# Six places of a hand-written order moved in a two-problem linear attention kernel

## The chip, the cores and the metric

The kernel runs on one core of one Trainium2 chip. Its time is the device time of one execution in microseconds (us). Engines are named as in the profile: PE multiplies matrices, PEld loads its weights, DVE works on vectors, ACT applies functions element by element and copies, POOL does some element-wise work and issues DMAs, SP issues DMAs. Each engine runs its own instructions in the order in which the program gives them to it, and waits on semaphores for the others.

## The reference, cut to what matters

Two independent problems, A and B, of 2048 tokens with 640 features each; 32 heads of 20 features. The results stand side by side in one output of 2048 x 1280.

```python
qkv = (x @ wqkv).reshape(B, S, 3, H, Dh)...          # q, k, v
phi = lambda t: jnp.where(t > 0, t + 1, jnp.exp(t)) + 1e-6
pq, pk = phi(q), phi(k)
kv  = jnp.einsum("bhsd,bhse->bhde", pk, v)
z   = jnp.einsum("bhsd->bhd", pk)
num = jnp.einsum("bhqd,bhde->bhqe", pq, kv)
den = jnp.einsum("bhqd,bhd->bhq", pq, z)[..., None] + 1e-6
out = concat_heads(num / den) @ wo
```

## The kernel before

**Numbers.** Every large product is made from float32 operands split into a rounded high part and a low part, which is the rest: ACT writes the high part, DVE subtracts it from the source for the low part (`split`, L1024; the subtraction waits in a list and is given to DVE by `flush`, L1019, at the next place of the order). A product is then three matrix products: high x high, high x low, low x high.

**Stages.** In the first half, up to about 283 us, the kernel makes phi(k) of both problems, the sums z, and per problem a 640 x 640 matrix M which holds kv and wo together. This half is ordered by a planner (`Plan`, L78) and is not touched by the change. M is turned into ten "forms" (forms 0 to 9: sums and differences of its blocks, each split high and low), with which an output product takes seven block products instead of eight.

The second half works on quarters of 512 tokens, numbered u = 0 to 7 (0 to 3 are A, 4 to 7 are B; NG = 4, NU = 8). For each quarter: q^T = wq^T x^T (`quarter`, `qmm`; for two quarters of each problem together `pair`, which uses sums of blocks of wq and x^T), phi of it (`qphi`: Exp and Relu on ACT out of a PSUM bank, then DVE; `qacc` adds up the denominators), a division (`divide`), sums of blocks and their splits (`d_sums`, `d_split`, `a_split`), and at last the output product with M (`outmm`). Sums over heads for the denominators go either through PE (`denmm`, quarter 0 alone) or through cross-partition copies, the foldings: `fold1`, `fold3`, `fold5` are copies on ACT, `fold2`, `fold4` additions and reciprocals on DVE.

PE's order in this half, with the start of each part in the profile of before: quarter 0; quarter 1; first part of pair 0, called p0 (326.5); output product 0 (337.0); second part of pair 0, called r0 (352.6); output product 1 (374.2); output product 2 (390.0); quarter 4 (406.9); output product 3 (423.9); quarter 5 (440.8); p1 (457.8); output product 4 (468.1); r1 (485.0); output products 5 (506.5), 6 (522.7) and 7 (538.5).

**The order by hand.** PE's work calls `run(slot)` after each small step, and `at(slot, f, ...)` hangs other work on a slot: `("q", u, c, k)` is after the three products k of column block c of quarter u; `("o", u, s)` is after step s (0 to 13) of output product u; `("p0", i, k)` and the like are steps of a pair. `run` first calls `flush`, then the functions hung there, in the order in which they were hung. A slot sets only the position in each engine's own list: an engine reaches the work when it has done what stands before it, and it may be ahead of PE or behind it.

**An output product** (`outmm`, L1357) has steps n = 0 to 6 for each half q of its 512 tokens. Step n = 0, 2, 4, 5 end with a copy of a PSUM bank into an output tile on ACT (L1396), n = 3, 4, 6 with an addition on DVE (L1397). PE goes on adding to the same bank after the copy, so step 2 waits for the copy of step 0, step 5 for that of step 4, and step 6 for the addition of step 4. The four output tiles `o` have four buffers (bufs=4); POOL (for the last product SP) stores them.

**What the change touches.**
- `chain` (L1662 on): a list per quarter of (slot, function). `chain[0]` is quarter 0 with its `denmm`; `early(b)` (L1667) is the quarter before the last of a problem; `chain[v]` (L1713) is the last quarter of all, v = 7, where `o` is output product 5 and `w` output product 6.
- `round_xq` (L1086): ACT rounds the high part of a piece of x^T for the next quarter from a staging tile; five pieces c = 0 to 4 per quarter. The low parts were made in the first half and are loaded (`load_xq`).
- `z_end` (L712, `finish`): four short DVE operations that finish z of problem B.
- `form_split`, `form_store` (L1145, L1151): six forms of B's M are split into tiles `fs` during quarter 4, stored to memory by POOL (L1156), and later loaded to where A's forms were (`form_load`). The tiles carry the tags `wo0` to `wo3` in turn: two per form, so every second form uses the same pair, and must wait until the store of the form before it in that pair has landed. Their order is 0, 2, 4, 6, 9, 8.
- `steps` (L1721): what a pair needs of wq and x^T. `tw_sums` (POOL) makes block sums of wq, `tw_split` (ACT, then DVE) splits them: `tw_split(b, 1, 1)` and `tw_split(b, 2, 0)` are the entries t[7] and t[9].

```python
parts = [base.tile([P, w], F32R, name=f"fs{t}", tag=turned("wo", 4), bufs=1) for t in "hl"]
o = [[q2[0].tile([P, 2, HF], F32, name="o", tag="o", bufs=4) for _ in range(2)] for _ in range(2)]
```

Of the kernel before, what the change touches and what calls it, by code (L numbers as in the profile page):

```python
# [9 lines left out]
F32R = mybir.dt.float32r  # L10
# [208 lines left out]
def tile_linear_attn_pair(ctx: ExitStack, tc: tile.TileContext, ins, out: bass.AP):  # L219
    nc = tc.nc  # L220
    P = 128
    S, D = ins[0]["x"].shape
    NC = D // P
    NT = S // P
    NG = NT // 4
# [9 lines left out]
    base = ctx.enter_context(tc.tile_pool(name="base", bufs=1))  # L235
# [5 lines left out]
    kx, kg, q1a, q1b, q2, q3 = [], [], [], [], [], []  # L241
# [450 lines left out]
    def zsums(b):  # L692

        z, zt32 = Space("zsum", D, ANY), Space("zturn", D, ANY)
        note("DVE", D, lambda: tt(z.all.f, zac[b][0].all.f, zac[b][1].all.f, op=OP.add), [z.all],
             [x.all for x in zac[b]] + ([G[1, NC - 1].all] if b else []), safe=6.0)
        part, four = Space("zpart", 20), Space("zfour", 20)
        pt, ft4 = zp[b]
        add = dict(axis=mybir.AxisListType.X, op=OP.add)
        note("DVE", D, lambda: nc.vector.transpose(zt32.all.f, z.all.f), [zt32.all], [z.all])  # L700
        note("DVE", D, lambda: nc.vector.tensor_reduce(
            pt.rearrange("p (g c) -> p c g", g=4), zt32.all.f.rearrange("p (c g t) -> p c g t", g=4, t=32), **add),
            [part.all], [zt32.all])
        zdv = Space("zd", 1)
        note("POOL", 1.0, lambda: nc.gpsimd.dma_start(zd[b], pt), [zdv.all], [part.all], dma=0.1, lat=2.0)
        for g in range(4):
            note("POOL", 1.0, lambda g=g: nc.gpsimd.dma_start(
                ft4[g * 32:g * 32 + 32].rearrange("p (q c) -> p q c", q=4),
                zd[b].rearrange("(q i) (g c) -> g i q c", q=4, g=4)[g]), [four[g:g + 1]], [zdv.all], dma=0.1, safe=6.0)
        zt, s = zz[b]  # L710

        def finish():  # L712
            nc.vector.tensor_reduce(zt, ft4.rearrange("p (q c) -> p c q", q=4), **add)
            nc.vector.tensor_scalar(zt, zt, S * EPS, None, op0=OP.add)
            nc.vector.tensor_reduce(s, zt, **add)
            nc.vector.tensor_scalar(s, s, EPS, EPS / 4, op0=OP.mult, op1=OP.add)

        if b == 0:
            note("DVE", 300, finish, [KZ[b].all], [four.all], safe=6.0)
        return finish  # L720
# [181 lines left out]
    for p in range(4, NPB):  # L902
        i, h = divmod(p - 2, 2)
# [9 lines left out]
    for p in range(NPB + 1, NP):  # L913
        if p == NPB + 1:
            fl = kvs
        else:
            i, h = divmod(p - NPB - 2, 2)
# [25 lines left out]
    z_end = zsums(1)  # L943
# [43 lines left out]
    for g, (h0, nh) in enumerate(GROUPS):  # L987
        cols = NC * DH * nh
        w = Space("wv", cols, (BD,))
# [23 lines left out]
    def turned(tag, n):  # L1013
        turn[tag] = (turn.get(tag, -1) + 1) % n
        return f"{tag}{places[turn[tag]] if tag == 'wst' else turn[tag]}"
# [8 lines left out]
    def split(hi, lo, src, now=False):  # L1024
        nc.scalar.activation(hi, src, AF.Copy)
        lows.append((lo, src, hi))
        if now:
            flush()
# [8 lines left out]
    def at(slot, f, *a):  # L1037
        todo.setdefault(slot, []).append((f, a))
# [103 lines left out]
    def width(i):  # L1142
        return D if i < 6 or i == 8 else HF

    def form_split(b, i):  # L1145
        w = width(i)
        parts = [base.tile([P, w], F32R, name=f"fs{t}", tag=turned("wo", 4), bufs=1) for t in "hl"]
        split(*parts, raw.pop((b, i))[:, :w])
        fd[b, i] = parts

# [453 lines left out]
    def forms2(b, places):  # L1604

        for i, a, s in places:
            at(a, form_split, b, i)
            at(s, form_store, b, i)
# [16 lines left out]
    h = NG - 1  # L1625
# [19 lines left out]
    for c in range(NC):  # L1645
        at(("q", 0, 4, c - 1) if c else ("q", 0, 3, 2), split_xq, 1, c, c == NC - 1)
        at(("o", 1, 8 + c // 2) if c < 2 else ("o", 2, c + 2), load_xraw, NG, c)
        at(("o", 1, 4 + c), load_xq, NG, c)
        at(("o", 2, 7 + c), round_xq, NG, c)
        u = NG  # L1650
        if c == 3:
            for k in (1, 3):
                at(("q", u, 3, 2), load_w, "m", 1, k)
        at(("q", u, *((3, 0), (3, 1), (3, 1), (4, 2), (4, 3))[c]), load_xraw, u + 1, c)
        at(("q", u, 4, c), load_xq, u + 1, c)
        at(("o", u - 1, (1, 2, 3, 11, 12)[c]), round_xq, u + 1, c)

    at(("o", 2, 8), z_end)

    den[0] = bank("psd", "small", 1)  # L1660

    chain = {  # L1662
        0: [(("q", 1, 0, 0), split_acc, 0), (("q", 1, 1, 1), denmm, 0), (("q", 1, 1, 1), recip, 0, 0),
            (("q", 1, 1, 1), recip, 0, 1), (("q", 1, 1, 2), divide, 0, 0), (("q", 1, 1, 4), divide, 0, 1),
            (("q", 1, 2, 0), d_sums, 0, 0), (("q", 1, 2, 2), a_split, 0, 0), (("q", 1, 2, 4), d_sums, 0, 1),
            (("q", 1, 3, 1), d_split, 0, 0), (("q", 1, 3, 4), a_split, 0, 1), (("q", 1, 4, 1), d_split, 0, 1)]}
    def early(b):  # L1667
        v = b * NG + NG - 1
        u = v - 1
        o, w, r = ("o", u - 1), ("o", u), (f"r{b}", 5)  # L1670
        y = (f"r{b}", 4)
        return [((*y, 4), phi7, v, 2), ((*y, 3), phi7, v, 3), ((*y, 1), fold1, u), ((*y, 2), fold2, u),
                ((*y, 2), qacc, v, 2), ((*r, 0), fold3, u, 0), ((*r, 0), fold3, u, 1), ((*r, 0), qacc, v, 3),
                ((*r, 1), fold4, u), ((*r, 1), phi7, v, 4), ((*r, 3) if b else (*o, 0), phi7, v, 0), ((*r, 3), qacc, v, 4),
                ((*o, 0) if b else (*o, 1), phi7, v, 1), ((*r, 5) if b else (*o, 1), qacc, v, 0), ((*o, 1) if b else (*o, 2), qacc, v, 1),
                ((*o, 2 - b), fold5, u, 0), ((*o, 2 - b), fold5, u, 1), ((*o, 3 - b), divide, u, 0), ((*o, 4 - b), divide, u, 1),
                *[((*w, n - 14) if n > 13 else (*o, n), f, u, i, q) for n, f, i, q in (
                    (9, d_sums, 0, 0), (10, a_split, 0, 0), (11, d_split, 0, 0), (11, d_sums, 1, 0), (12, a_split, 1, 0),
                    (13, d_split, 1, 0), (14, d_sums, 0, 1), (15, a_split, 0, 1), (16, d_split, 0, 1), (16, d_sums, 1, 1),
                    (17, a_split, 1, 1), (19, d_split, 1, 1))]]  # L1680

    for v in range(1, NU - 2):
# [3 lines left out]
        w, u = v - 1, v + 1  # L1686
# [6 lines left out]
        if v == NU - 3:  # L1693
            p = "p1"
# [14 lines left out]
    u, v = NU - 2, NU - 1  # L1709
    o, w = ("o", u - 1), ("o", u)  # L1710
    chain[u] = early(1)
    e = ("o", v)
    chain[v] = [((*o, 4), fold1, v), ((*o, 5), fold2, v), ((*o, 8), fold3, v, 0), ((*o, 8), fold3, v, 1),  # L1713
                ((*o, 10), fold4, v, 0), ((*w, 4), fold4, v, 1), ((*w, 6), fold5, v, 0), ((*w, 7), fold5, v, 1),
                ((*w, 6), divide, v, 0), ((*w, 7), divide, v, 1),
                *[((*e, n - 14) if n > 13 else (*w, n), f, v, i, q) for n, f, i, q in (
                    (8, d_sums, 0, 0), (9, a_split, 0, 0), (10, d_split, 0, 0), (10, d_sums, 1, 0), (11, a_split, 1, 0),
# [3 lines left out]
    def steps(b, t, x, n0):  # L1721
        p, r, o = f"p{b}", f"r{b}", ("o", b * NG + NG - 4)
        X = [(n0 + i) % 6 for i in range(6)]
        for a, f, *y in ((t[0], tw_load, b, 0), (t[1], tw_sums, b, 0), (t[2], tw_split, b, 0, 0), (t[3], tw_split, b, 0, 1),
                         (t[4], tw_load, b, 1), (t[5], tw_sums, b, 1), (t[6], tw_split, b, 1, 0), (t[7], tw_split, b, 1, 1),
                         ((p, 0, 0), tw_load, b, 2, X[5]), (t[8], tw_sums, b, 2), (t[9], tw_split, b, 2, 0)):
            at(a, f, *y)
        for a, f, *y in ((x[0], xload, 0, 0, X[0]), (x[1], xload, 0, 1, "o"), (x[2], xload, 0, 2, "o"), (x[3], xload, 0, 3, X[1]),
                         (x[4], xload, 0, 4, X[2]), ((p, 0, 0), xsum, 1, 0, X[3]), ((p, 0, 1), xsum, 1, 1, X[4]),
                         ((*o, 0), xsum, 0, 0, X[5]), ((p, 1, 0), xsum, 0, 1, X[0]), ((p, 1, 1), xsum, 2, 0, X[1]),  # L1730
                         ((p, 1, 2), xsum, 2, 1, "w"), ((p, 1, 2), xload, 1, 4, X[2]),
                         ((r, 0, 0), xsum, 3, 0, "o"), ((r, 0, 0), xsum, 3, 1, X[3]), ((r, 0, 1), xload, 0, 4, X[4]),
                         ((r, 1, 0), xload, 1, 3, X[5]), ((r, 1, 1), xload, 1, 0, X[0]), ((r, 1, 1), xload, 1, 1, "o"),
                         ((r, 2, 3), xload, 1, 2, X[1])):
            at(a, f, b, *y)

    p, h = "p1", NU - 3
    X0, X1 = [(turn["xqh"] + 1 + NC * i) % 6 for i in (1, 3)]
    steps(1, (("q", h, 0, 4), ("q", h, 2, 0), ("q", h, 3, 0), ("q", h, 3, 2), ("q", h, 4, 2), (p, 0, 0), (p, 1, 1), (p, 1, 2),
              (p, 1, 0), (p, 1, 2)),  # L1740
          (("q", h, 0, 3), ("q", h, 1, 1), ("q", h, 1, 2), ("q", h, 4, 0), ("q", h, 4, 1)), X1)
    p = "p0"
    steps(0, (("q", 0, 4, 4), ("q", 1, 0, 3), ("q", 1, 1, 2), ("q", 1, 2, 1), ("q", 1, 3, 0), (p, 0, 1), (p, 1, 0), (p, 1, 2),
# [83 lines left out]
```

## Time and profile before

| | before |
|---|---|
| runs (us) | 558.67, 559.19, 560.62 |
| median (us) | 559.19 |
| profiled execution, its own time (us) | 559.77 |
| its span, first to last instruction (us) | 558.0 |
| busy in the span (us): PE, PEld, DVE, ACT, POOL | 550.9, 495.3, 435.7, 355.4, 94.9 |
| granted TensorE clock | 1.00 throughout |

A row of the timeline gives start and duration in us, engine, line of the kernel, operation, out<-in by tile names, sizes, count, and in brackets the idle time of the engine before it with what ended it. Names: `psq`, `psd`, `pa`, `pe`, `psb` are PSUM banks; `xqh` high parts of x^T; `fsh`, `fsl` the split forms and `fdh`, `fdl` their place in memory; `twh`, `twl` split parts of wq; `ac`, `rd` denominators; `o` output tiles. Matrix products overlap in PE, so their pace is read from their starts, not from their durations.

### The profile page before, as it was taken

The numbers are of one execution on the slowest core, as the hardware profiler recorded it, in microseconds if no ns is written. First come the engines' busy times: TensorE is split into PE (matmuls) and PEld (weight loads), VectorE is DVE, ScalarE is ACT, GpSimd is POOL, SyncE is SP. The second block draws the span as 40 slices with busy tenths as digits, with TensorE's granted clock in tenths as the row PEclk, the third lists the DMA queues.
The fourth block names the chain that finished last, engine by engine and source line by source line (L and its number), as shares of the span: only waits on it lengthen the run. The fifth ranks groups of instructions, "written<-read, shape, count | busy, mean of one in ns | idle before, by whom it ended". The sixth has DMA issues, their size and how long they took to land.

```text
span 558.0 us, 9441 instructions
## 1 busy us (share of the span) xinstructions
PE 550.9 (99%) x3342; PEld 495.3 (89%) x3342; DVE 435.7 (78%) x708; ACT 355.4 (64%) x671; POOL 94.9 (17%) x145
## 2 busy tenths in 40 slices
PE   9999999999999999999999999999999999999997
PEld 7999999998998889998887789889988988989997
DVE  7788777579887576978774799779797878959992
ACT  6777476574667656657345557487866856558661
POOL 1210111101211111101214530101333323100110
PEclk9999999999999999999999999999999999999999
DMA  8785998979859989999999979748467986670222
GB/s 317 268 217 168 233 297 228 291 214 280 251 158 258 298 221 314 310 355 286 309 312 272 365 248 323 266 145 288 155 227 241 314 317 208 211 260 1 95 96 94
DMA packets 96359, 135.48 MB, mean 243 GB/s; under 512 B 8248, under 2 KB 54232, under 8 KB 96312
## 3 DMA queue, kind: packets, MB, share of 16 engines
q1 hardware_dynamic: 87000, 108.55, 59.9%
q0 software_dynamic: 9024, 25.94, 17.2%
q8 instruction: 26, 0.43, 0.3%
q10 hardware_dynamic: 288, 0.39, 0.2%
q14 instruction: 21, 0.17, 0.1%
HBM read 79.58 MB, written 44.78 MB: 223 GB/s over the span
## 4 chain that ended last, share of the span: by engine, by line
PE 85%; issue 4%; DMA 3%; ACT 2%; DVE 2%; POOL 2%; SPq 0%; POOLq 0%; ACTq 0%
PE psg L565 20%; PE ka L315 10%; PE pa L1381 10%; PE psq L1526 10%; PE ke L315 5%; PE psr L565 5%; PE pe L1381 5%; PE psk L831 4%; PE psb L1381 3%; PE kb L315 3%; PE psq L1031 2%; PE psq L1032 2%; PE psq L1033 2%; PE pskv L620 1%; PE psm L633 1%
## 5 line engine op out<-in xcount | busy, mean ns | idle before, releaser
L565 PE MATMUL psg<-pkh,xnl 128*128 128x512 f32 x160 | 63.0, 394 | 0.0
L565 PE MATMUL psg<-pkl,xnh 128*128 128x512 f32 x160 | 63.0, 394 | 0.0
L565 PE MATMUL psg<-pkh,xnh 128*128 128x512 f32 x160 | 62.5, 391 | 0.0
L417 POOL DMA_DIRECT2D zacc<-ek x32 | 26.2, 818 | 199.7 <-DVE ek L521 168.9
L511 ACT ACTIVATE kt<-ka 128x320 f32<-128x320 f32 x52 | 22.5, 433 | 55.3 <-PE ka L315 55.1
L1396 ACT ACTIVATE o<-pa 128x320 f32<-128x320 f32 x64 | 27.7, 439 | 30.4 <-PE pa L1381 27.4
L1218 DVE SCALAR_TENSOR_TENSOR pq<-eq,rq 128x512 f32<-128x512 f32 x40 | 28.1, 711 | 11.2 <-ACT rq L1217 11.1
L565 PEld LDWEIGHTS psg<-pkh,xnl 128*128 128x128 f32 x160 | 30.1, 188 | 6.5
L1031 PE MATMUL psq<-xqh,wh 128*128 128x512 f32 x90 | 35.5, 394 | 0.0
L1032 PE MATMUL psq<-xql,wh 128*128 128x512 f32 x90 | 35.2, 391 | 0.0
L1033 PE MATMUL psq<-xqh,wl 128*128 128x512 f32 x90 | 35.1, 390 | 0.0
L565 PEld LDWEIGHTS psg<-pkh,xnh 128*128 128x128 f32 x160 | 30.1, 188 | 4.8
L565 PEld LDWEIGHTS psg<-pkl,xnh 128*128 128x128 f32 x160 | 30.1, 188 | 4.8
L521 DVE SCALAR_TENSOR_TENSOR ek<-ek,kt 128x640 f32<-128x640 f32 x26 | 21.4, 822 | 15.8 <-ACT kt L520 15.8
L412 ACT ACTIVATE pkh<-ek,epst 128x640 fp32r<-128x640 f32 x32 | 26.5, 828 | 6.8 <-DVE ek L521 6.6
L578 DVE TENSOR_TENSOR gacc<-psg,gacc 128x512 f32<-128x512 f32 x30 | 20.6, 688 | 11.0 <-PE psg L565 10.9
L413 DVE SCALAR_TENSOR_TENSOR pkl<-ek,pkh 128x640 fp32r<-128x640 f32 x32 | 26.2, 821 | 3.6 <-ACT pkh L412 3.5
L1229 DVE SCALAR_TENSOR_TENSOR acc<-pq,z,acc 128x512 f32<-128x512 f32 x32 | 26.0, 813 | 1.5 <-ACT acc L1227 0.5
L1434 POOL DMA_DIRECT2D out<-o x14 | 7.7, 549 | 113.7 <-ACT o L1396 81.2
L1381 PE MATMUL pa<-fm,dah 128*128 128x320 f32 x112 | 26.5, 311 | 0.3 <-ACT o L1396 0.3
L309 DVE TENSOR_TENSOR xnl<-xns,xnh 128x640 fp32r<-128x640 f32 x32 | 25.7, 819 | 0.9 <-ACT xnh L306 0.8
L309 DVE TENSOR_TENSOR xl<-xts,xh 128x640 fp32r<-128x640 f32 x29 | 23.8, 821 | 2.7 <-ACT xh L306 2.5
(270 smaller groups left out, 1834.5 us busy)
## 6 DMA issues: line engine op xcount, KB each, us to landing
zacc<-ek POOLq DMA_DIRECT2D x32, 320.0 KB, 5.5
out<-o POOLq DMA_DIRECT2D x28, 320.0 KB, 3.3
xd<-xl SPq DMA_DIRECT2D x24, 320.0 KB, 3.7
xql<-xd SPq DMA_DIRECT2D x26, 256.0 KB, 6.0
xns<-in_A_x SPq DMA_DIRECT2D x16, 320.0 KB, 6.3
xh<-xh SPq DMA_DIRECT2D x16, 320.0 KB, 4.0
xts<-in_B_xt_tiles SPq DMA_DIRECT2D x16, 320.0 KB, 4.4
xns<-in_B_x SPq DMA_DIRECT2D x16, 320.0 KB, 6.8
```

The lines of the kernel that those rows point to most:

```text
L309: note("DVE", n, lambda: tt(lo.r, src.f, hi.f, op=OP.subtract), [lo], [src, hi], ahead=10.0)
L315: nc.tensor.matmul(o, a.r, w.r, start=start and k == i == 0, stop=k == n - 1 and i == 2, skip_group_check=True)
L412: note("ACT", n + 110, lambda: act(hi.r, p.f, AF.Identity, bias=epst), [hi], [p, K0.all], by=8.0)
L413: note("DVE", n, lambda: stt(lo.r, p.f, EPS, hi.f, op0=OP.add, op1=OP.subtract), [lo], [p, hi], by=9.0)
L565: nc.tensor.matmul(o[:, :n], a.r, w.r, start=j == 0 and q == 0, stop=j == 2 and q == 2, skip_group_check=True)
L1031: nc.tensor.matmul(o, whi, xhi, start=first, stop=False)
L1032: nc.tensor.matmul(o, whi, xlo, start=False, stop=False)
L1033: nc.tensor.matmul(o, wlo, xhi, start=False, stop=last)
L1218: nc.vector.scalar_tensor_tensor(pq[u][:, c, :], e, 1.0, r, op0=OP.min, op1=OP.add)
L1381: nc.tensor.matmul(ps, x, y, start=start and n == i == 0, stop=n == len(terms) - 1 and i == 2, skip_group_check=True)
L1396: copy = lambda x, y: nc.scalar.activation(x, y, AF.Copy)
L1526: nc.tensor.matmul(ps, a, z, start=first and i == 0, stop=last and i == 2, skip_group_check=True)
```

## The change

Six places of the order move. Nothing is computed that was not computed before, and no instruction is added or removed.

1. Quarter 0's `denmm` and its two reciprocals go from slot ("q", 1, 1, 1) to ("q", 1, 1, 2), and its first `divide` from there to ("q", 1, 1, 3).
2. The five roundings of quarter 4's x^T go from steps 7, 8, 9, 10, 11 of output product 2 to steps 2, 4, 9, 11, 13; `z_end` goes from step 8 of that product to the second part of p0.
3. Forms 4 and 6 of B are split into two tiles each of the output ring `o` instead of the `wo` tiles; forms 9 and 8 thereby take the `wo` tiles that forms 0 and 2 had.
4. In the last-but-one quarter of B, the second `divide` goes from step 3 to step 7 of output product 5.
5. For the last quarter, in output product 5: `fold1` from step 4 to 3, `fold2` from 5 to 4, the halves of `fold3` from 8 and 8 to 5 and 7, the first half of `fold4` from 10 to 8.
6. `tw_split(1, 1, 1)` and `tw_split(1, 2, 0)` go from the end of p1 to steps 3 and 2 of output product 4.

```diff
     def form_split(b, i):
         w = width(i)
-        parts = [base.tile([P, w], F32R, name=f"fs{t}", tag=turned("wo", 4), bufs=1) for t in "hl"]
+        if b and i in (4, 6):
+            parts = [q2[0].tile([P, D], F32R, name=f"fs{t}", tag="o", bufs=4)[:, :w] for t in "hl"]
+        else:
+            parts = [base.tile([P, w], F32R, name=f"fs{t}", tag=turned("wo", 4), bufs=1) for t in "hl"]
...
-        at(("o", 2, 7 + c), round_xq, NG, c)
+        at(("o", 2, (2, 4, 9, 11, 13)[c]), round_xq, NG, c)
...
-    at(("o", 2, 8), z_end)
+    at(("p0", 1, 0), z_end)
...
-        0: [(("q", 1, 0, 0), split_acc, 0), (("q", 1, 1, 1), denmm, 0), (("q", 1, 1, 1), recip, 0, 0),
-            (("q", 1, 1, 1), recip, 0, 1), (("q", 1, 1, 2), divide, 0, 0), (("q", 1, 1, 4), divide, 0, 1),
+        0: [(("q", 1, 0, 0), split_acc, 0), (("q", 1, 1, 2), denmm, 0), (("q", 1, 1, 2), recip, 0, 0),
+            (("q", 1, 1, 2), recip, 0, 1), (("q", 1, 1, 3), divide, 0, 0), (("q", 1, 1, 4), divide, 0, 1),
...
-... ((*o, 3 - b), divide, u, 0), ((*o, 4 - b), divide, u, 1),
+... ((*o, 3 - b), divide, u, 0), ((*o, 4 + 3 * b), divide, u, 1),
...
-    chain[v] = [((*o, 4), fold1, v), ((*o, 5), fold2, v), ((*o, 8), fold3, v, 0), ((*o, 8), fold3, v, 1),
-                ((*o, 10), fold4, v, 0), ((*w, 4), fold4, v, 1), ...
+    chain[v] = [((*o, 3), fold1, v), ((*o, 4), fold2, v), ((*o, 5), fold3, v, 0), ((*o, 7), fold3, v, 1),
+                ((*o, 8), fold4, v, 0), ((*w, 4), fold4, v, 1), ...
...
-    steps(1, (..., (p, 0, 0), (p, 1, 1), (p, 1, 2),
-              (p, 1, 0), (p, 1, 2)),
+    steps(1, (..., (p, 0, 0), (p, 1, 1), ("o", h - 1, 3),
+              (p, 1, 0), ("o", h - 1, 2)),
```

More of the change, by code (lines that the diff above doesn't have):

```diff
@@ L1675, in early @@
                 ((*o, 0) if b else (*o, 1), phi7, v, 1), ((*r, 5) if b else (*o, 1), qacc, v, 0), ((*o, 1) if b else (*o, 2), qacc, v, 1),
-                ((*o, 2 - b), fold5, u, 0), ((*o, 2 - b), fold5, u, 1), ((*o, 3 - b), divide, u, 0), ((*o, 4 - b), divide, u, 1),
+                ((*o, 2 - b), fold5, u, 0), ((*o, 2 - b), fold5, u, 1), ((*o, 3 - b), divide, u, 0), ((*o, 4 + 3 * b), divide, u, 1),
                 *[((*w, n - 14) if n > 13 else (*o, n), f, u, i, q) for n, f, i, q in (
@@ L1712, in tile_linear_attn_pair @@
     e = ("o", v)
-    chain[v] = [((*o, 4), fold1, v), ((*o, 5), fold2, v), ((*o, 8), fold3, v, 0), ((*o, 8), fold3, v, 1),
-                ((*o, 10), fold4, v, 0), ((*w, 4), fold4, v, 1), ((*w, 6), fold5, v, 0), ((*w, 7), fold5, v, 1),
+    chain[v] = [((*o, 3), fold1, v), ((*o, 4), fold2, v), ((*o, 5), fold3, v, 0), ((*o, 7), fold3, v, 1),
+                ((*o, 8), fold4, v, 0), ((*w, 4), fold4, v, 1), ((*w, 6), fold5, v, 0), ((*w, 7), fold5, v, 1),
                 ((*w, 6), divide, v, 0), ((*w, 7), divide, v, 1),
@@ L1738, in tile_linear_attn_pair @@
     X0, X1 = [(turn["xqh"] + 1 + NC * i) % 6 for i in (1, 3)]
-    steps(1, (("q", h, 0, 4), ("q", h, 2, 0), ("q", h, 3, 0), ("q", h, 3, 2), ("q", h, 4, 2), (p, 0, 0), (p, 1, 1), (p, 1, 2),
-              (p, 1, 0), (p, 1, 2)),
+    steps(1, (("q", h, 0, 4), ("q", h, 2, 0), ("q", h, 3, 0), ("q", h, 3, 2), ("q", h, 4, 2), (p, 0, 0), (p, 1, 1), ("o", h - 1, 3),
+              (p, 1, 0), ("o", h - 1, 2)),
           (("q", h, 0, 3), ("q", h, 1, 1), ("q", h, 1, 2), ("q", h, 4, 0), ("q", h, 4, 1)), X1)
```

## The prediction

> **What bounds the kernel now.** I read the page's busy times first, then the chain of waits in order of time, then the list of who waited for whom on PE, and last the timeline around each of those waits.
>
> ```profile
> PE 550.9 (99%) x3342; PEld 495.3 (89%) x3342; DVE 435.7 (78%) x708; ACT 355.4 (64%) x671; POOL 94.9 (17%) x145
> ```
> ```profile
> 337.00 1.76 PE pa L1381 x12
> ...
> 485.15 21.54 PE psq L1526 x93
> ```
> ```profile
> PE pa L1381 <- ACT o L1396: 0.8, 2, 0.6
> PE pe L1381 <- ACT rq L1217: 0.8, 1, 0.8
> PE psd L1240 <- DVE ac L1022: 0.6, 1, 0.6
> PE pe L1381 <- DVE o L1397: 0.3, 1, 0.3
> ```
>
> The first row says that PE is the bound: 550.9 of 558.0 us. The chain gives its pace: 1.76/12 = 0.147 us from one 320-column product to the next, 21.54/93 = 0.23 us for 512 columns. A product's own row shows 0.31 or 0.39 us, so successive products overlap, and an idle time in brackets is less than what PE loses: I add 0.31 - 0.147 = 0.16 us to it. The last four rows are every wait of PE over 0.15 us behind the start-up. No product is added or removed by the change, so it can gain only what these waits cost, and lose only by new ones.
>
> **The change part by part.**
>
> *First denominators (denmm, recip, divide of quarter 0).*
>
> ```profile
> 312.91 0.39 PE L1239 MATMUL psd<-ac,same 128*128 128x512 f32 x1
> 313.90 0.50 PE L1240 MATMUL psd<-ac,same 128*128 128x512 f32 x1 [0.61 <-DVE ac L1022]
> 314.24 0.39 PE L1031 MATMUL psq<-xqh,wh 128*128 128x512 f32 x1
> ```
>
> The second product comes 0.99 us after the first instead of 0.23: a loss of 0.76. The next comes after 0.34, so refilling PE costs another 0.11; I use that for every wait. The low half of the sums is ready at 313.9 whatever PE does. With denmm one step later, three products (3 x 0.23 = 0.69) stand ahead of it, and 0.07 us of wait stays. The gain is between 0.69 and 0.87, and I take 0.75. The reciprocals start when both sums are in, which is at the same time as now; DVE and ACT therefore do not come earlier here, only PE does. The tw_split's low half now goes ahead of the first divide on DVE, a swap of two operations inside one backlog.
>
> *z_end, out of output product 2 and into the pair's first part (p0).* Four short DVE operations, the first the longest:
>
> ```profile
> 399.62 0.19 DVE L713 TENSOR_REDUCE z<-zq 128x5 f32<-128x20 f32 x1
> ```
> ```profile
> 338.22 0.69 DVE L1218 SCALAR_TENSOR_TENSOR pq<-eq,rq 128x512 f32<-128x512 f32 x1 [0.68 <-ACT rq L1217]
> ```
>
> Four times 0.19 is 0.76 at most. In their new place they run just ahead of the second row, where DVE idles 0.68 us for an ACT result that is paced by PE; that idle time covers them but for 0.1, and it is also where the backlog that the denominators left is worked off. Without this cover the pair's additions would be 0.76 later; I cost it at nothing.
>
> *Roundings of x^T in output product 2.*
>
> ```profile
> 402.99 0.31 PE L1381 MATMUL pe<-fm,dal 128*128 128x320 f32 x1
> 403.57 0.56 PE L1381 MATMUL pa<-fm,dah 128*128 128x320 f32 x2 [0.27 <-ACT o L1396]
> ```
> ```profile
> 400.69 0.84 ACT L1265 ACTIVATE ac<-ac 32x256 f32<-32x256 f32 x2
> 401.56 0.63 ACT L1088 ACTIVATE xqh<-xqs 128x512 fp32r<-128x512 f32 x1
> 402.21 0.84 ACT L1265 ACTIVATE ac<-ac 32x256 f32<-32x256 f32 x2
> 403.08 0.44 ACT L1396 ACTIVATE o<-pa 128x320 f32<-128x320 f32 x1
> ```
> ```profile
> 403.08 0.98 DVE L1270 TENSOR_TENSOR ac<-ac 128x256 f32<-128x256 f32 x1 [1.88 <-ACT ac L1265]
> 404.10 0.95 DVE L1272 RECIPROCAL ac<-ac 128x128 f32<-128x128 f32 x1
> ```
>
> PE loses 0.58 - 0.147 = 0.43 at 403.57, and 0.30 + 0.16 = 0.46 at the next wait, the one on DVE; with two refills that is 1.1 us. ACT runs in order: the copy PE needs stands at 403.08 behind roundings and foldings. The change puts two of the five roundings into steps 2 and 4, so about 2 x 0.63 goes from ahead of these foldings, less a wait for PE in between; the foldings end near 402.05 and the copy near 402.5, before PE's own 402.99 + 0.147 = 403.14. DVE follows: sum and reciprocal (0.98 + 0.95) end near 404.0, the addition behind them near 404.45, and PE wants it after nine products at 404.47. So the first wait goes whole and the second but for 0 to 0.15. The last rounding is now behind the foldings at the product's end; the next quarter uses it only in its fifth part, 12 x 0.23 = 2.8 us later, and it and the half folding ahead of it take 1.5. Gain 0.95 to 1.1; I take 1.0.
>
> *Two M forms in output tiles.*
>
> ```profile
> 422.70 0.61 ACT L1217 ACTIVATE rq<-psq 128x512 f32<-128x512 f32 x1
> 426.05 0.74 ACT L1025 ACTIVATE fsh<-wst 128x640 fp32r<-128x640 f32 x1 [2.75 <-DVE fsl L1022]
> ```
> ```profile
> 428.14 0.42 PE L1381 MATMUL pa<-fh,dsh 128*128 128x320 f32 x1 [0.55 <-ACT o L1396]
> ```
> ```profile
> 419.45 0.54 POOL L1156 DMA_DIRECT2D fdh<-fsh  x1
> ```
> ```profile
> L1156 POOL DMA_DIRECT2D fdh<-fsh x6: 540/540/542, 409.5 to 427.1; - x6
> ...
> DMA to landing us min/median/max: 2.4/4.4/6.5
> ```
> ```profile
> 425.08 0.49 DVE L1022 TENSOR_TENSOR fsl<-t,fsh 128x320 fp32r<-128x320 f32 x1 [3.06 <-DMA fdl<-fsl]
> ```
>
> ACT stands still for 2.75 us before splitting form 8. That split goes into one of the four wo tiles that form 6 used before, so form 6's store must land first: issued at 419.45, landed after 6.5 us at the longest, 425.95, which fits 426.05. (The row names a DVE operation, but that one ended at 425.08 + 0.49 = 425.57.) Behind this split stand the last exponentials of quarter 4 and output product 3's copies; PE pays 0.55 + 0.16 at 428.14, with the refill 0.82. With forms 4 and 6 in o tiles, forms 9 and 8 get the wo tiles of forms 0 and 2, whose stores are the first of the group, from 409.5 on, and ACT's wait is gone. What is late next: output product 3's copies write o tiles, and now wait for the stores of forms 4 and 6. The first copies are needed at PE's step 5, 0.88 after 427.43, less the 1.0 gained above: 427.3. The copy takes 0.44, so form 6's store must have landed by 426.8; at 425.95 that leaves 0.85. The gain lies between 0 and 0.95 (a later wait at 436 goes partly too); I take 0.8.
>
> DMA: Bandwidth & Descriptors of the Trainium skill (section "Issuing engines are not separate DMA queues") says that transfers of all issuing engines run on the same 16 DMA engines and interleave, which speaks against this part: SP's loads for the next quarter are released by PE, come 1 us earlier, and would share with the store. The trace agrees in so far as these landings spread from 2.4 to 6.5 us. By the rows alone the sum below stays; by that rule a landing 1.5 us later would take 0.65 off it.
>
> *Parts of wq (tw_split).*
>
> ```profile
> 471.72 0.42 PE L1381 MATMUL pe<-fh,dsh 128*128 128x320 f32 x1 [0.77 <-ACT rq L1217]
> ```
> ```profile
> 469.59 0.91 ACT L1025 ACTIVATE twh<-wqr 128x256 fp32r<-128x256 f32 x3
> 470.41 0.29 ACT L1025 ACTIVATE twl<-wqr 128x128 fp32r<-128x128 f32 x1
> 470.61 0.57 ACT L1216 ACTIVATE eq<-psq 128x512 f32<-128x512 f32 x1
> 471.08 0.58 ACT L1217 ACTIVATE rq<-psq 128x512 f32<-128x512 f32 x1
> ```
>
> PE's loss: 0.77 + 0.16, and 0.1: 1.03. Output product 4 needs the bank that the Exp and Relu at 470.61 and 471.08 read. The four splits ahead of them, 469.59 to 470.61 = 1.02 us, go behind; Relu would end at 470.64, and PE wants it at 471.72 - 0.93 = 470.79. The work is not gone but stands in steps 2 and 3, ahead of the next copies:
>
> ```profile
> 475.91 0.44 ACT L1396 ACTIVATE o<-pa 128x320 f32<-128x320 f32 x1
> ```
> ```profile
> 477.10 0.31 PE L1381 MATMUL pa<-fh,dsh 128*128 128x320 f32 x1
> ```
>
> If ACT is as late as now, this copy again ends at 476.35 while PE, freed of the wait, wants it at 477.10 - 1.03 = 476.07: 0.3 lost there and some 0.2 at the next, and only 0.4 of 1.03 stays. If ACT comes earlier, as it should when form 8's block of 2.75 us no longer delays what SP and POOL load for these parts, all of it stays. Bounds 0.4 and 1.03; I take 0.75, nearer the upper end.
>
> *Last foldings and a divide apart (output product 5).*
>
> ```profile
> 518.27 0.31 PE L1381 MATMUL pa<-fm,dal 128*128 128x320 f32 x1
> 518.66 0.56 PE L1381 MATMUL pa<-fm,dah 128*128 128x320 f32 x2
> ```
> ```profile
> 516.44 1.70 ACT L1265 ACTIVATE ac<-ac 32x256 f32<-32x256 f32 x4
> 518.17 0.89 ACT L1396 ACTIVATE o<-pa 128x320 f32<-128x320 f32 x2
> ```
>
> PE loses 0.39 - 0.147 = 0.24, with refill 0.34, behind four foldings of 1.70 in one place. Two of them move three steps ahead, two one step, and the divide behind them on DVE. Fold1, one step earlier, now stands ahead of a copy with little to spare; bounds -0.1 and 0.34; I take 0.25.
>
> **Sum.** 0.75 + 1.0 + 0.8 + 0.75 + 0.25 = 3.55, of 0.87 + 1.1 + 0.82 + 1.03 + 0.34 = 4.2 that there is. The profiled execution took 559.77 us by its own time (its span is 558.0, 1.8 lie around it), so that one would become 556.2. The median of the runs, 559.19, is 0.58 under it; the same step gives 555.7.
>
> **The rivals.**
> (1) *ACT becomes the bound in output product 4*: the displaced splits cost there, 0.4 instead of 1.03 (row 475.91). With the other parts as taken that is 3.2, about 556.0; with the first copy of product 3 also late, 2.6, or 556.6. For it speaks that ACT has no bracketed wait from 469.59 to 471.08; against it, that ACT's work before that place is released by loads that come earlier.
> (2) *The gains are swallowed*: the denominators show that DVE and ACT stay at their times while PE comes earlier. Where such a chain lasts until the next wait, PE only waits there instead. If only the first denominators and half the roundings' gain last, 0.75 + 0.5 = 1.25 remains: 557.9. Against it stands DVE's 0.68 of idle time at 338.22, and 1.88 at 403.08.
> (3) *Slower: form 6's store holds the output tile*. From 426.8 each us that it lands later is a us of PE. Past 430.35 the whole 3.55 is eaten; a store that took 13 us, twice the longest, would land at 432.45, cost 5.65, and end 2.1 above the kernel before: 561.3. The longest of twelve is 6.5, so little speaks for it.
> (4) *The change does not free ACT*: if the block at 426.05 were DVE's, as the row names, and not the store's, 0.8 falls away: 556.4. DVE itself waited for a store just before, 3.06 us at 425.08, of the same four tiles, so the change would free it too.
>
> **How the numbers follow.** The forecast, 555.7 (555.0 to 556.3), 0.50; rivals (1) 0.22, (4) 0.10, (2) 0.14, (3) 0.04. 0.3% is 1.7 us, about what a measurement of this kernel tells from no change. The forecast, (1) and (4) gain more than that: faster 0.82. (2) counts as the same: 0.14. Slower 0.04. The low end is all 4.2 gone and 0.4 of scatter: 554.6. The high end takes in (2): 558.0.
>
> **What would show it.** Right: no wait of PE at the second denominator product over 0.2; none on ACT or DVE in output product 2; ACT going on to form 8's split with no wait, and product 3's second copy not waiting for a store; Relu of the pair's fifth block ending before product 4's fourth step; a span near 554.5. Wrong: a PE wait in product 3 released by a DMA through ACT, a PE wait on an o copy in steps 8 and 9 of product 4, or any PE wait in output product 0, where z_end and the backlog meet.

## The result and the profile after

| | before | after |
|---|---|---|
| median of the runs, us | 559.25 (558.67 to 560.62) | 556.65 (555.87 to 556.90) |
| profiled execution: own time, span | 559.77, 558.0 | 556.65, 554.9 |

The ratio of the times is 0.9949, with a 95% interval of 0.9937 to 0.9962: the changed kernel is faster by 2.6 us. Two runs of kernels further down, 1100.67 us of *wq back* and 772.45 us of *forms alone*, lie far from all others, and the ratios leave them out. 555.7 was forecast, with a range of 554.6 to 558.0. Between the two profiled executions lie 3.1 us. The prediction took 0.58 off for the distance of the profiled execution from the median; the execution of after has no such distance, so half a microsecond of the miss is the choice of the execution and not of the kernel.

In the kernel after, lines of the code from L1148 on stand three further down (L1381 is L1384). The first fence is the page's busy times, the second the whole list of PE's waits (us in total, times, longest):

```profile
PE 549.9 (99%) x3342; PEld 494.7 (89%) x3342; DVE 435.5 (78%) x708; ACT 355.1 (64%) x671; POOL 94.9 (17%) x145
```
```profile
PE psi L745 <- DVE ones L323: 1.0, 1, 1.0
PE psk L804 <- ACT xjh L306: 0.4, 1, 0.4
```

Both rows belong to the start-up. All five listed waits of the kernel before behind the start-up are gone. What PE still loses there is below the list's bound, and is seen only where a product starts later than the pace allows. The timelines of these places follow. First denominators:

```profile
312.91 1.27 DVE L1022 TENSOR_TENSOR ac<-acc,ac 128x512 fp32r<-128x512 f32 x1 [0.70 <-ACT ac L1025]
313.80 0.39 PE L1242 MATMUL psd<-ac,same 128*128 128x512 f32 x1
314.10 1.22 DVE L1221 SCALAR_TENSOR_TENSOR pq<-eq,rq 128x512 f32<-128x512 f32 x1
314.23 0.50 PE L1243 MATMUL psd<-ac,same 128*128 128x512 f32 x1
314.57 0.39 PE L1031 MATMUL psq<-xqh,wh 128*128 128x512 f32 x1
```

The second product comes 0.43 after the first instead of 0.23: 0.20 is lost, and 0.10 with the refill behind it, where there were 0.87. In p0 there is a loss that was not there before; the load it waits for stands behind another one on SP's queue:

```profile
325.06 0.81 SPq L1458 DMA_DIRECT2D wqr<-in_A_wq  x2
325.98 0.37 SPq L1497 DMA_DIRECT2D xo<-xh  x1
326.45 0.37 SPq L1497 DMA_DIRECT2D xo<-xd  x1
```
```profile
330.29 0.92 PE L1529 MATMUL psq<-xo,wh 128*128 128x512 f32 x2
331.04 0.39 PE L1529 MATMUL psq<-xo,wl 128*128 128x512 f32 x1
```

Two products from 330.29 take 0.92 instead of 0.63, and the next starts 0.75 behind instead of 0.46: 0.29 in all. Output product 2, where PE lost 1.1, is clean:

```profile
400.68 0.63 ACT L1088 ACTIVATE xqh<-xqs 128x512 fp32r<-128x512 f32 x1
401.34 0.84 ACT L1268 ACTIVATE ac<-ac 32x256 f32<-32x256 f32 x2
402.21 0.44 ACT L1399 ACTIVATE o<-pa 128x320 f32<-128x320 f32 x1
```
```profile
403.09 0.46 PE L1384 MATMUL pa<-fm,dah 128*128 128x320 f32 x2
```

The copy that PE needs ends at 402.65, ahead of the product into the next bank at 403.09, and two products take 0.46, which is the pace. ACT no longer stands still ahead of form 8:

```profile
421.41 0.62 ACT L1220 ACTIVATE rq<-psq 128x512 f32<-128x512 f32 x1
421.89 0.77 ACT L1025 ACTIVATE fsh<-wst 128x640 fp32r<-128x640 f32 x1
```

In output product 4 the wait on Relu is gone, and a small one on an o copy has come, behind the splits that were moved (rival 1 in small):

```profile
467.64 0.59 ACT L1220 ACTIVATE rq<-psq 128x512 f32<-128x512 f32 x1
...
473.05 0.72 ACT L1025 ACTIVATE twh<-wqr 128x256 fp32r<-128x256 f32 x2
473.68 0.42 ACT L1399 ACTIVATE o<-pa 128x320 f32<-128x320 f32 x1
```
```profile
473.84 0.31 PE L1384 MATMUL psb<-fm,dal 128*128 128x320 f32 x1
474.15 0.41 PE L1384 MATMUL pa<-fh,dsh 128*128 128x320 f32 x1
```

It costs 0.31 - 0.147 = 0.16, and 0.1 with the refill. Added up, what is gone is 0.57 (denominators), 1.1 (roundings), 0.8 (form 8), 0.77 (Relu, less the new 0.26) and 0.34 (last foldings), and 0.29 in p0 is new: 3.3. The start of the second half lay 0.2 later in this execution, which leaves the 3.1.

### The profile page after: what moved, and what is told of

It is laid out like the page before. It is cut to its first block, busy times and chain, and to the rows that moved or that the text cites. A ratio compares the mean times of both kernels' runs of the same rounds, so it can differ in the third digit from the quotient of the medians.

```text
span 554.9 us, 9447 instructions
## 1 busy us (share of the span) xinstructions
PE 549.9 (99%) x3342; PEld 494.7 (89%) x3342; DVE 435.5 (78%) x708; ACT 355.1 (64%) x671; POOL 94.9 (17%) x145
## 4 chain that ended last, share of the span: by engine, by line
PE 98%; DMA 1%; DVE 0%; ACT 0%; SPq 0%; issue 0%
PE psg L565 20%; PE pa L1384 13%; PE psq L1529 12%; PE ka L315 10%; PE pe L1384 6%; PE ke L315 5%; PE psr L565 5%; PE psk L831 4%; PE psq L1031 4%; PE psb L1384 4%; PE psq L1032 4%; PE psq L1033 4%; PE kb L315 3%; PE pskv L620 1%; PE psm L633 1%; DMA xj<-in_A_xt 1%
## 5 line engine op out<-in xcount | busy, mean ns | idle before, releaser
L1232 DVE SCALAR_TENSOR_TENSOR acc<-pq,z,acc 128x512 f32<-128x512 f32 x32 | 26.3, 822 | 1.5 <-ACT acc L1230 0.5
L1384 PE MATMUL pa<-fm,dah 128*128 128x320 f32 x112 | 26.3, 309 | 0.0
```

The source lines that it names most:

```text
L1232: nc.vector.scalar_tensor_tensor(acc[u], p, z, acc[u], op0=OP.mult, op1=OP.add)
L1384: nc.tensor.matmul(ps, x, y, start=start and n == i == 0, stop=n == len(terms) - 1 and i == 2, skip_group_check=True)
```

## The experiments

Single executions differ in their first half, which no edit here touches: the first product of quarter 1 starts between 308.0 and 309.8 us. Each ratio is to runs of the kernel before that were made alongside (their medians are 559.45 to 559.67), so kernels are better compared by the ratios than by the medians. Beside the ratio (with its interval) the table gives the span behind that product in the profiled execution, which is where the edits act.

| kernel | median, us | ratio (95%) | behind, us | PE's losses there over 0.25 us, refill included |
|---|---|---|---|---|
| before | 559.25 | | 250.0 | 0.87, 0.52, 0.56, 0.82, 1.03, 0.34 |
| after | 556.65 | 0.9949 (0.9937 to 0.9962) | 246.6 | 0.30, 0.29, 0.26 |
| forms back | 558.42 | 0.9974 (0.9962 to 0.9985) | 247.8 | 0.48, 1.31, 0.28 |
| wq back | 556.23 | 0.9940 (0.9916 to 0.9963) | 246.2 | 0.35 |
| roundings back | 557.85 | 0.9964 (0.9952 to 0.9977) | 247.5 | 0.40, 0.27, 0.53, 0.57 |
| foldings back | 556.60 | 0.9942 (0.9922 to 0.9961) | 247.0 | 0.37, 0.34 |
| z_end back | 556.84 | 0.9954 (0.9940 to 0.9968) | 246.0 | 0.26 |
| denominators alone | 560.11 | 1.0008 (0.9996 to 1.0019) | 250.6 | 0.42, 0.53, 0.55, 0.97, 1.73, 0.34 |
| POOL's sums later | 556.47 | 0.9950 (0.9936 to 0.9965) | 246.0 | 0.26 |
| xo first | 555.86 | 0.9937 (0.9924 to 0.9950) | 245.7 | none |
| forms alone | 558.44 | 0.9981 (0.9971 to 0.9991) | 248.7 | 1.06, 0.53, 0.55, 0.50, 0.33 |
| form 4's store late | 556.17 | 0.9943 (0.9931 to 0.9955) | 246.5 | 0.26, 0.51 |
| form 6's store late | 557.87 | 0.9971 (0.9960 to 0.9981) | 247.4 | 0.36, 0.30, 0.63 |
| three edits together | 561.03 | 1.0022 (1.0005 to 1.0038) | 249.1 | 0.26, 1.84, 1.27 |

*Forms back* (undo the third part of the change):

```diff
-        if b and i in (4, 6):
+        if False:
```


> The changed kernel with forms 4 and 6 of M again in wo tiles; all else stays. Theory (each part is worth the wait that it removes): ACT again stands still some 2.7 us before it splits form 8, ending where a store of form 6 lands, and PE waits on an o copy in output product 3 for 0.7 to 0.8: 557.4 against 556.65. Rival (4), the block is DVE's and not the store's: no idle time of ACT at form 8, or none that costs: 556.7. Rival (2), gains are swallowed: ACT's block is back, but PE loses under 0.3.

```profile
425.24 0.74 ACT L1025 ACTIVATE fsh<-wst 128x640 fp32r<-128x640 f32 x1 [2.75 <-DVE fsl L1022]
```
```profile
PE pa L1384 <- ACT o L1399: 1.0, 1, 1.0
```

The block is back, and rival (4) falls: the tiles were its cause. But it costs PE 1.31, not 0.82. It ends only 0.81 earlier than in the kernel before, while PE, freed of the waits ahead of it, comes some 1.3 earlier and stands there longer. So this part is worth more with the others than by itself. No wait on Relu has come back.

*wq back* (undo the sixth part):

```diff
-... (p, 1, 1), ("o", h - 1, 3), (p, 1, 0), ("o", h - 1, 2) ...
+... (p, 1, 1), (p, 1, 2), (p, 1, 0), (p, 1, 2) ...
```


> The changed kernel with the last parts of wq split again in the pair's first part, ahead of the Exp and Relu of its fifth block. Theory: the wait of PE on Relu before output product 4's fourth step is back (0.93 with refill, and 0.1), and the wait on the o copy at 474.15 (0.16 and 0.10) goes: 0.7 to 0.8 more, 557.4. Rival (1), ACT is the bound there: what the one wait costs the other gives back, 556.7 to 556.9.

```profile
466.09 0.91 ACT L1025 ACTIVATE twh<-wqr 128x256 fp32r<-128x256 f32 x3
...
467.58 0.58 ACT L1220 ACTIVATE rq<-psq 128x512 f32<-128x512 f32 x1
```

The four splits are again ahead of Exp and Relu, and PE does not wait: neither for Relu nor for the copy at 474. Relu ends at 468.16. A mark for where PE stands is ACT's Exp of the third block of quarter 5, which waits for PE: it starts at 449.10 here and at 451.26 in the kernel before. So PE stands 2.16 earlier and wants Relu at 470.79 - 2.16 = 468.63. Both theories of the expectation fall: nothing was lost by undoing this part. Where did ACT find the time? The first suspects were the loads. Here are SP's rows for wq and that Exp, of the kernel before and of the kernel after:

```profile
446.66 1.19 SPq L1455 DMA_DIRECT2D wqr<-in_B_wq  x2
...
451.26 0.60 ACT L1216 ACTIVATE eq<-psq 128x512 f32<-128x512 f32 x1 [1.13 <-PE psq L1033]
```
```profile
443.07 1.21 SPq L1458 DMA_DIRECT2D wqr<-in_B_wq  x2
...
449.20 0.60 ACT L1219 ACTIVATE eq<-psq 128x512 f32<-128x512 f32 x1 [1.12 <-PE psq L1033]
```

The load goes out 4.60 ahead of the Exp before, 6.13 after. In the three kernels then at hand with the forms in wo tiles the lead was 4.1 to 4.6, in seven with them in output tiles 5.5 to 6.3. That made a new theory: the forms, not wq's parts, had removed the wait on Relu too. (The expectation that follows calls this Exp the last one of the pair's first part; it belongs to quarter 5.)

*Forms alone* (only the third part, on the kernel before) tests it:

> The kernel before with forms 4 and 6 alone in output tiles. Theory now (the late store of form 8 also kept back SP's loads, so that the loads of wq's rows in the pair's first part were issued 4.1 to 4.6 us ahead of that part's last Exp and are issued 5.5 to 6.3 ahead with the forms in output tiles): besides the wait in output product 3 (0.82) the wait on Relu in output product 4 (1.03) goes as well, with wq's parts where they were: 1.6 to 1.9 less, 557.6 against 559.4. The prediction's sum: 0.8 less, and the wait on Relu stays: 558.6.

```profile
PE pe L1384 <- ACT rq L1220: 0.2, 1, 0.2
```

The wait in output product 3 is gone, and the loss at Relu is 0.50 instead of 1.03 (the kernel gains 1.26 us behind the first product, 1.1 by the ratio). But the lead of wq's load, 5.09, is not what did it: ACT's first split of wq starts 4.87 behind the Exp here (455.94) as in the kernel before (456.13). The time lies later, in DVE's last two operations of quarter 5. ACT waits for them before its foldings, and from there to Relu it runs without a wait. Rows of the kernel before, of *forms alone* and of *wq back*:

```profile
462.89 1.23 DVE L1218 SCALAR_TENSOR_TENSOR pq<-eq,rq 128x512 f32<-128x512 f32 x1
464.16 1.11 DVE L1229 SCALAR_TENSOR_TENSOR acc<-pq,z,acc 128x512 f32<-128x512 f32 x1
465.30 0.42 ACT L1251 ACTIVATE ac<-acc 64x256 f32<-64x256 f32 x1 [4.00 <-DVE acc L1229]
```
```profile
462.71 0.69 DVE L1221 SCALAR_TENSOR_TENSOR pq<-eq,rq 128x512 f32<-128x512 f32 x1
463.43 1.11 DVE L1232 SCALAR_TENSOR_TENSOR acc<-pq,z,acc 128x512 f32<-128x512 f32 x1
```
```profile
460.28 0.69 DVE L1221 SCALAR_TENSOR_TENSOR pq<-eq,rq 128x512 f32<-128x512 f32 x1
461.00 0.75 DVE L1232 SCALAR_TENSOR_TENSOR acc<-pq,z,acc 128x512 f32<-128x512 f32 x1
```

The long ones started while a sum of POOL was running (the sums start at 462.83, 463.22 and 461.24 in these three), the short ones did not. In *forms alone* the first is 0.54 shorter than before, and that is the 0.53 that PE gains at Relu. In *wq back* both are short, 0.90 in all, and ACT's first split comes 4.41 behind the Exp instead of 4.87. So the foldings start 12.69 behind the Exp instead of 14.04.

How early is early enough? With the four splits ahead of it, Relu ends 6.37 after the foldings start, in all three, and PE wants it 470.79 - 451.26 = 19.53 behind the Exp. So by estimate the foldings have to start within 19.53 - 6.37 = 13.16. In nine of the ten profiled kernels that have the forms in output tiles together with other parts both operations of DVE are short, and the foldings start 12.4 to 12.8 behind: early enough without the move. The execution of the kernel after is the tenth. Its second operation took 1.28, and the foldings start 13.67 behind; without the move Relu would have come 0.5 too late there. So the new theory is half right: with the forms in output tiles ACT comes early enough in most executions, but more by which operations of DVE and POOL meet than by the load's lead. Whether the forms decide that is not shown by one profile of each kernel.

*Roundings back*, with z_end left in p0:

```diff
-        at(("o", 2, (2, 4, 9, 11, 13)[c]), round_xq, NG, c)
+        at(("o", 2, 7 + c), round_xq, NG, c)
```


> The changed kernel with the five roundings of x^T again in five successive steps of output product 2 (z_end stays in p0). Theory: both waits of output product 2 are back, on ACT's o copy and on DVE's addition, 1.0 to 1.1 more: 557.7. Rival (2), swallowed: the waits come back but a later wait (434.90) shrinks with them, so that 0.5 or less remains: 557.2. Third: without z_end's four operations DVE is earlier, and only the first wait (0.43 and refill) is back.

Both waits are back at their old size (0.53 and 0.57). The first theory holds: 1.1 for this part at its place. The stretch behind the first product is 0.9 longer than in the kernel after, as the small wait on the o copy in output product 4 (0.26) is not there in this execution.

*z_end back* in output product 2:

```diff
-    at(("p0", 1, 0), z_end)
+    at(("o", 2, 8), z_end)
```


> The changed kernel with z_end again in output product 2, ahead of that product's last foldings. Theory (z_end is free at either place, as its four operations of 0.76 us in sum lie in DVE's idle time): no PE wait comes or goes, 556.65. Rival: in p0 it stood behind a backlog and cost the additions there 0.7, so that without it the load of xo or the additions come earlier and PE's wait at 330.70 shrinks, 0.1 to 0.3 less; or it delays DVE's sum in output product 2 and up to 0.4 comes back there.

No wait appears in output product 2, and the times of the two kernels can't be told apart. z_end is free at either place. (There was no wait for xo in this execution, but none in that of wq back either, where z_end is in p0.)

*Foldings back*:

```diff
-((*o, 3), fold1, v), ((*o, 4), fold2, v), ((*o, 5), fold3, v, 0), ((*o, 7), fold3, v, 1), ((*o, 8), fold4, v, 0)
+((*o, 4), fold1, v), ((*o, 5), fold2, v), ((*o, 8), fold3, v, 0), ((*o, 8), fold3, v, 1), ((*o, 10), fold4, v, 0)
```
(and the divide at step 3 again)

> The changed kernel with the last foldings and the divide of output product 5 where they were. Theory: PE loses 0.24 and a refill of 0.10 at the copy behind four foldings: 557.0. Rival: fold1, one step earlier, cost as much elsewhere as the spreading gained, so that no waits differ in sum: 556.65.

PE loses 0.24 and 0.10 again at 515.91, as expected. The runs' times don't show so little: 556.60.

*Denominators alone*, on the kernel before:

```diff
-(("q", 1, 1, 1), denmm, 0), ... recip ... (("q", 1, 1, 2), divide, 0, 0)
+(("q", 1, 1, 2), denmm, 0), ... recip ... (("q", 1, 1, 3), divide, 0, 0)
```


> The kernel before with the first denominators alone one step later. Theory: PE's 0.87 (wait and refill) at the second denominator product shrinks to the 0.07 of the arithmetic plus a refill if DVE is as in the kernel before, or to 0.3 if POOL's sums of wq collide with DVE's operations as in the changed kernel's profile: 0.57 to 0.75 less than before; and at the load of xo in p0 PE gains or loses by how late DVE is, 0 to 0.3. So 558.4 to 558.9 against 559.25. Rival (2), swallowed: DVE's chain is not earlier, and PE gives all of it back in p0: 559.25.

```profile
PE pe L1381 <- ACT rq L1217: 1.5, 1, 1.5
...
PE psq L1526 <- DMA xql<-xd: 0.2, 1, 0.2
```

The wait at the denominators is gone, all but a refill of 0.11, and yet the kernel is no faster. Of the 0.76 gained, 0.19 goes at the load of xo in p0 and 0.42 into a new wait for a load later in the pair (the last row), so that in output product 2 PE is only 0.06 ahead (403.51 against 403.57). This is rival (2): alone, this part's gain is swallowed. The losses at form 8's block and at Relu are 0.15 and 0.70 greater than in the profile of before. At Relu the delay begins with the load of wq, for which POOL's first sum waits: it starts at 454.42 instead of 453.75, with the Exp at 451.26 in both. Whether that is the edit's doing or this execution's own can't be said from one profile.

*POOL's sums later* asks why the low half of the sums was late in the kernel after:

```diff
-(("q", 0, 4, 4), ("q", 1, 0, 3), ("q", 1, 1, 2), ("q", 1, 2, 1), ...
+(("q", 0, 4, 4), ("q", 1, 1, 3), ("q", 1, 2, 0), ("q", 1, 2, 1), ...
```


> The changed kernel with POOL's sums for the first parts of wq behind the first denominators in the order (and the split that reads them two steps later). Theory (POOL's sums slow DVE where both run): qacc of quarter 0's neighbour takes 0.75 in place of 1.23 us, ac's low half 0.63 in place of 1.27 and pq 0.68 in place of 1.22; the second denominator product does not wait any more (0.30 less), and the xo load in p0 goes out earlier as the split that its queue waits for comes earlier (0 to 0.29 less): 556.1 to 556.4. Rival: those durations are DVE's own and do not change; then the waits stay, 556.65, or grow as the split is two steps later: up to 557.0.

DVE's and POOL's rows of this kernel:

```profile
311.00 0.75 DVE L1232 SCALAR_TENSOR_TENSOR acc<-pq,z,acc 128x512 f32<-128x512 f32 x1
312.45 1.27 DVE L1022 TENSOR_TENSOR ac<-acc,ac 128x512 fp32r<-128x512 f32 x1 [0.70 <-ACT ac L1025]
313.64 1.22 DVE L1221 SCALAR_TENSOR_TENSOR pq<-eq,rq 128x512 f32<-128x512 f32 x1
```
```profile
311.56 0.79 POOL L1469 TENSOR_TENSOR wqx<-wqr 128x256 f32<-128x256 f32 x1
312.43 0.75 POOL L1470 TENSOR_TENSOR wqr<-wqr 128x256 f32<-128x256 f32 x1
313.25 1.06 POOL L1471 TENSOR_TENSOR wqx<-wqr 128x256 f32<-128x256 f32 x1
```

The sums did not move far, as POOL waits for nothing that PE does; they only went behind some stores. The first of the three DVE operations ran almost clear of them and took 0.75 instead of 1.23, the other two met a sum and took 1.27 and 1.22, where the kernel *xo first*, whose sums were over by 312.7, shows 0.69 for both. So the durations are POOL's doing, as the theory said; the low half came early enough, and the wait at the denominators is gone. The page SBUF — State Buffer of the Trainium skill (section "Who interferes with whom") says that a DVE operation with two inputs in SBUF and a GpSimd one that reads SBUF exclude each other; these rows agree. The other half of the theory does not hold: xo's load in p0 went out 0.46 earlier than in the kernel after (325.52 and 325.98), but PE came 0.27 earlier too, and 0.26 is still lost there.

*xo first*:

```diff
-(("q", 1, 0, 2), ("q", 1, 2, 1), ("q", 1, 3, 0), ("q", 1, 4, 0), ...
+(("q", 1, 0, 2), ("q", 1, 2, 1), ("q", 1, 2, 4), ("q", 1, 4, 0), ...
```


> The changed kernel with the load of xo for the third part of p0 ahead of the load of wq's rows on SP's queue. Theory (xo is late because it stands behind a load that waits for DVE's low half of twl): xo lands some us earlier and PE's wait at 330.70 (0.18 and 0.11) is gone: 556.35. Rival: xo waits for something else, its tile's last use or the DMA engines, and lands as late as now: 556.65.

```profile
320.67 0.32 SPq L1497 DMA_DIRECT2D xo<-xd  x1
324.26 0.81 SPq L1458 DMA_DIRECT2D wqr<-in_A_wq  x2
```

xo's second half goes out 5.8 earlier, and its wait is gone: it only stood behind a load that waited for DVE. In this execution PE waits for nothing behind the start-up. 555.86 (555.61 to 556.10) is the lowest median here; the runs of after lie from 555.87 to 556.90. The intervals of the two ratios overlap, so the gain over the kernel after is seen in the profile and not shown by the times.

*The two stores* test rival (3), with form 6's (in the first kernel form 4's) store put further back in POOL's order:

```diff
-(4, ("q", NG, 1, 2), ("q", NG, 1, 4)), (6, ("q", NG, 2, 0), ("q", NG, 2, 2))
+(4, ("q", NG, 1, 2), ("q", NG, 3, 4)), ...       first kernel
+..., (6, ("q", NG, 2, 0), ("q", NG, 4, 4))       second kernel
```


> The changed kernel with form 4's store behind the stores of forms 6 and 9 in POOL's order, issued some 4 us later. Theory (the first two copies of output product 3 write the tiles that form 4's two halves left): its low half lands at 428 to 429.5, the second copy ends 0.44 later against 427.19 that PE needs, so PE waits 1.2 to 2.8 there: 557.9 to 559.4 against 556.65. By rival (3) as recorded, form 6's tiles are the first to be written, and form 4's store may land then: 556.65.

> The changed kernel with form 6's store behind form 8's in POOL's order, issued some 8 us later, at 427.1. Theory (form 6's tiles are first written by the copies at 432.2 and 434.2): it lands at 430.7 to 434, PE wants the first of these copies to end by some 433.5, so 0 to 0.9 is lost: 556.65 to 557.5. Rival (3) as recorded: from 426.8 each us is a us of PE, 4 to 7 lost: 560.5 or more.

Form 4's store can be late at no cost in output product 3 (the 0.51 of the table is xo's wait in p0): my theory of fixed tiles was wrong. In the waits of that program the first copies take the tiles of form 6, whose store now goes out ahead of form 4's: the program hands tiles on in the order in which they are let go. With form 6's store behind form 8's, the second pair of tiles is the late one:

```profile
428.84 0.54 POOL L1159 DMA_DIRECT2D fdh<-fsh  x1
```
```profile
434.81 0.44 ACT L1399 ACTIVATE o<-pa 128x320 f32<-128x320 f32 x1 [1.70 <-DMA fdh<-fsh]
```
```profile
437.25 0.56 PE L1384 MATMUL pa<-fm,dah 128*128 128x320 f32 x2 [0.37 <-ACT o L1399]
```

A copy waits 1.70 for the landing, which ends with the copy's start at 434.81, and PE loses 0.30 and 0.63. The mechanism of rival (3) exists, but its point of decision is wrong: by 426.8 (428.4 in this execution, whose second half starts 1.6 later) the price would have been over 6 us. These tiles are wanted only by the second pair of copies.

*Three edits together* (POOL's sums later, xo first, and wq's larger parts in step 6 of output product 4 instead of 3) were to be the best kernel:

```diff
-... (p, 1, 1), ("o", h - 1, 3), ...
+... (p, 1, 1), ("o", h - 1, 6), ...
```


> The changed kernel with POOL's sums behind the first denominators, xo's load ahead of that of wq's rows, and the last high and low parts of wq's form in output product 4 at step 6 instead of 3. Theory: no wait of PE but that of the start-up is left, in whatever execution: 555.6 to 556.0, a span of 553.9. Rival: the moved sums and splits collide with DVE's or ACT's work at a new place (the divides of quarter 0, the additions of p0), and a wait of 0.2 to 0.5 comes back: 556.2.

DVE's low half of the split, SP's rows, and the two products that wait:

```profile
476.40 0.75 DVE L1022 TENSOR_TENSOR twl<-wqr,twh 128x256 fp32r<-128x256 f32 x2
```
```profile
477.21 0.32 SPq L1502 DMA_DIRECT2D xw<-xsh  x1
477.58 1.39 SPq L1502 DMA_DIRECT2D xw<-xsl  x1
...
480.43 0.47 SPq L1502 DMA_DIRECT2D xql<-xsl  x1
```
```profile
486.81 0.50 PE L1529 MATMUL psq<-xqh,twh 128*128 128x512 f32 x1 [1.67 <-DMA xqh<-xsh]
488.21 0.50 PE L1529 MATMUL psq<-xql,twh 128*128 128x512 f32 x1 [0.90 <-DMA xql<-xsl]
```

Its median lies above that of the kernel before, and the profile shows a cause that neither theory named. wq's split reads a tile into which SP loads xw next. That load goes out when the low half is done (476.40 + 0.75 = 477.15). SP runs in order, so xw (477.21, where it was 474.32 in the kernel before and 470.82 with wq back) holds the loads behind it, and the last two are needed at 485. The sixth part of the change itself spends this slack: in the kernel after xw goes out at 475.07, while PE comes 2 us earlier.

These waits cost PE 1.84 and 1.27, 3.1 in all, which takes the kernel after to some 559.8; the profiled execution took 559.71. They do not explain the whole median: the four runs with a granted clock of 0.999 or 1.000 took 558.02 to 559.71, no more than the kernel before, and the eight with 0.993 to 0.997 took 560.27 to 563.32. Why the clock was lower in these is open.

## Why the prediction was right, point by point

- **Denominators**, 0.75 of 0.87: 0.57 came. The step that failed is "0.07 us of wait stays": 0.20 stayed. The operations that make the low half met POOL's sums in both kernels, but the first of them (L1229, now L1232) took 1.23 us instead of 1.11, and so the low half came 0.11 later behind the start of quarter 1. That the gain lasts is owed to the other parts; alone it is swallowed, as rival (2) had it.
- **z_end** at nothing: confirmed by putting it back. The wait that appeared in p0 (0.29) is another: xo's load, behind wq's on SP. The prediction has no term for this one: it considered DVE there and not SP's queue.
- **Roundings**, 1.0 (0.95 to 1.1): 1.1, step by step as worked out.
- **Forms**, 0.8 (0 to 0.95): put in alone they remove the 0.82, as priced. With the other parts in place they are worth more: undone, they cost 1.31 at the same place, since the block's end moves less than PE does. With them the load of wq goes out earlier (5.1 to 6.3 ahead of the Exp in eleven kernels, 4.1 to 4.6 in three without).
- **wq's parts**, 0.75 (0.4 to 1.03): the times show no gain. The prediction saw that ACT comes earlier once form 8's block is gone, but counted this for the move instead of asking whether it made the move needless, and it did not consider the sums of POOL that DVE meets there. In the executions of the kernel after and of *forms back* ACT is late (foldings 13.67 and 13.69 behind the Exp), and there the move keeps Relu in time; in most others it is not needed. The prediction priced the splits among ACT's copies (0.26 came) and overlooked the loads behind xw.
- **Foldings**, 0.25: 0.34.
- **The sum**, 3.55: 3.3 between the executions, and 2.6 between the medians. That it fits so well is partly luck. The terms were not independent: taken out of the whole, the forms are worth 0.5 more than their term and wq's parts up to 0.75 less, and the 0.29 in p0 was not in the sum. (559.19 less 3.55 is 555.64, which the prediction gives as 555.7.)
- **Rivals and signs**: (1) happened in small, in two executions of those profiled (0.26 and 0.28), and with it came one of the prediction's signs of being wrong, a PE wait on an o copy in step 8 of output product 4; (2) holds for the denominators alone, not for the whole; (3) is a mechanism that exists, but its point lies more than 5 us later than it was put; (4) falls.

## What to carry to other kernels

Terms that are each worked out against the profile of before overlap where one of them frees a blocked engine: ask of every later term whether the wait would still be there, and take parts out of the whole as well as putting them in alone. Where two engines slow each other, what a part seems to gain in one execution can come from operations that happen to miss each other. A wait whose end is set by a transfer need not move with the bound engine; while it stands, part of what is gained ahead of it is lost in it. And of a step that is moved, ask which load writes next into what it reads, and what stands behind that load in its queue: three steps later, on top of the change's own move, cost 3.1 us of PE's time here.

## What the runs showed of the hardware

The DVE operations of 128x512 shown in these rows, with two inputs in SBUF, took 0.68 to 0.75 us alone and 1.11 to 1.28 when they started while one of POOL's sums was running, and those sums took 0.72 to 0.75 alone and up to 1.29 beside DVE. Which of them meet differs from execution to execution, as POOL waits for loads (its first sum in quarter 1 started at 308.67, 309.81 and 310.92 in three kernels with the same order up to it). That goes into the scatter, with a first half that ends between 308.0 and 309.8, and parts of 0.3 us do not show in the times.
